# Attention and FFN in one kernel: 12 FFN chunks of 384 tokens instead of 9 of 512, four PSUM work banks, and another order of the attention's steps

## The chip, the cores and the metric

One core of one Trainium2 chip runs the whole kernel. The metric is the device time of one launch in microseconds, less being better. The core has TensorE (PE in the profile; PEld is its weight load), VectorE (DVE), ScalarE (ACT), GpSimd (POOL) and SyncE (SP), which issues all the DMAs here. Matrix products go to PSUM, eight banks of 512 float32 per partition.

## The reference

```
# q, k, v: (8 batches, 8 heads, 576 positions, 64); blocks of 64 positions
scores = q @ k^T / 8;  masked where block(row) < block(column)
attn = exp(scores - max); attn = attn / (sum + 1e-9)
x = (attn @ v) as (4608 tokens, 512)
h = x @ w_in                                  # w_in (512, 2048)
g = h if h >= 1, 0 if h <= -1, else (h + 1)^2 / 4
out = g @ w_out                               # w_out (2048, 512)
```

All of it is float32. The kernel computes with float32r operands and splits a float32 value into a high and a low part where it wants more precision: a product is then the sum of two or three matmuls (high x high, low x high, high x low).

## The kernel before

**Attention.** A `Pair` is two heads of one batch; there are 32 pairs, four to a batch. `attention_steps` walks over them in eight steps each, and every step ends with a `yield`. A pair needs `scores(j, g)` for its two heads j and three groups g of query rows (matmuls into a work bank, VectorE's maximum, ScalarE's exponential with its sum, VectorE's reciprocal and scaling), `scores_last` for the last 64 rows of both heads, `turn` and `turn_last` (TensorE transposes of the probabilities, then a copy to a high and a subtraction to a low part), and three parts of attn*v: `attn_v_first` for the first 256 rows of both heads, `attn_v(0)` and `attn_v(1)` for the rest. `add_halves` adds the two halves of a result (ScalarE copy, VectorE addition), and `store_x` writes x, split in high and low, into a ring of 1,536 tokens, `xh` and `xl`. From batch 1 on (`hop`) the probabilities go through a DMA, `as_float32r`, to a second buffer `prr` before they are turned; there are three buffers of the tag `bits` for that. From batch 2 on (`far`, also `raw`) an old pair's last parts run in the first steps of the next pair, and q and k come by way of `fetch` (a copy in DRAM), `load_qk`, `turned` and `turned_last` (TensorE transposes and `parted`). Batches 0 and 1 (`plain`) use plain float32 for attn*v and another order of steps, the `else` branches.

**FFN.** `feed_forward` goes over chunks of `TCH` = 512 tokens and, in each, over 16 slices `fc` of the hidden dimension. `ffn_in` makes one slice of h: 12 matmuls into the single bank `ph`, then ScalarE `t`, VectorE `t` twice, ScalarE `gh`, GpSimd `gl`, and a DMA of the slice of w_out, `wo`. `ffn_out` adds that slice to `po`, one bank for each 128 tokens: 8 matmuls with `gh` (L794) and 4 with `gl` (L799). The order is in(0), in(1), out(0), in(2), out(1) and so on; each of these is called an FFN block here. Two `wo`, `gh` and `gl` buffers exist.

**Order.** The main loop at the end runs the attention's steps; from step `START` = 36 on it issues one FFN block after each step, and when the attention is over, the rest of the blocks. `prepare_weights` converts the weights from float32 to their two parts, 64 pieces, in the early steps: 24 pieces by step 36 and the others in the 24 steps after it. The tile framework makes the instruction streams from this program order: it takes program order as priority and lets an instruction pass another that is not ready by its own estimate, which is why an attention transpose stands inside an `out` block in places. Each engine then runs its stream in order, and waits on semaphores.

**PSUM.** `ps_w` has 3 banks (`work_bank`: scores, transposes, attn*v), `ps_h` 1 (`ph`), `ps_o` 4 (`po`). Until step 36 `work_bank` also uses the `po` banks, every other time.

## Time and profile before

| | |
|---|---|
| median of 3 runs | 1270.7 us (1269.4 to 1272.47) |
| profiled execution | 1269.69 us, span 1267.9 us |
| mean granted TensorE clock | 0.981 |
| TensorE busy | 1200.1 us, 6280 matmuls |
| VectorE, ScalarE, GpSimd busy | 887.0, 703.2, 394.6 us |
| chain that ended last | PE 69%, DVE 16%, ACT 6%, issue 5% |
| DMA | 215.43 MB, mean 170 GB/s |

The profile is of one execution. Its parts are busy times, 40 slices of the span, the chain of work that ended last, groups of instructions by line and shape (busy us, mean ns of one, idle before it and what ended that), and DMA issues. A timeline row gives start, duration, engine, line, operation, result and operands, shape, count, and in brackets the idle time before it with its releaser. The ends of matmuls are modelled, so that two matmuls in a row overlap in the records; the distance between two starts shows how fast they go. A wait row says who waited for whom, us in total, times, and the longest.

### The profile page before, as it was taken

The numbers are of one execution on the slowest core, as the hardware profiler recorded it, in microseconds if no ns is written. First come the engines' busy times: TensorE is split into PE (matmuls) and PEld (weight loads), VectorE is DVE, ScalarE is ACT, GpSimd is POOL, SyncE is SP. The second block draws the span as 40 slices with busy tenths as digits, with TensorE's granted clock in tenths as the row PEclk, the third lists the DMA queues.
The fourth block names the chain that finished last, engine by engine and source line by source line (L and its number), as shares of the span: only waits on it lengthen the run. The fifth ranks groups of instructions, "written<-read, shape, count | busy, mean of one in ns | idle before, by whom it ended". The sixth has DMA issues, their size and how long they took to land.

```text
span 1267.9 us, 20253 instructions
## 1 busy us (share of the span) xinstructions
PE 1200.1 (95%) x6280; PEld 998.8 (79%) x6280; DVE 887.0 (70%) x2188; ACT 703.2 (55%) x1827; POOL 394.6 (31%) x430
## 2 busy tenths in 40 slices
PE   5888889899999999999999999999999999999998
PEld 4666667678888888888888888888888888888886
DVE  8898877758777777777777777787777777322222
ACT  5787656646566655665656655566556555222222
POOL 3555655522222222222222222222222222222222
PEclk9888988999999999999999999999999999999999
DMA  5566666667888655555554655465556433422432
GB/s 158 167 176 215 203 228 197 217 198 237 260 273 266 215 162 158 154 175 163 156 162 145 187 157 152 138 189 153 160 154 190 137 128 118 132 87 98 133 100 100
DMA packets 185259, 215.43 MB, mean 170 GB/s; under 512 B 113840, under 2 KB 132272, under 8 KB 184384
## 3 DMA queue, kind: packets, MB, share of 16 engines
q1 hardware_dynamic: 185152, 214.14, 54.9%
q8 instruction: 50, 0.82, 0.3%
q14 instruction: 57, 0.47, 0.1%
HBM read 134.74 MB, written 31.98 MB: 131 GB/s over the span
## 4 chain that ended last, share of the span: by engine, by line
PE 69%; DVE 16%; ACT 6%; issue 5%; DMA 1%; POOL 1%; SPq 1%; ACTq 0%; POOLq 0%; DVEq 0%
PE ph L770 29%; PE po L794 15%; PE po L799 7%; PE ps_av L591 7%; PE ps_s L482 4%; ACT pr L509 3%; PE ps_s L485 3%; DVE t L780 2%; PE ps_t L552 2%; DVE t L783 2%; ACT t L779 2%; DVE pb L547 2%; DVE nm L505 2%; DVE sm L491 1%; DVE pr L515 1%
## 5 line engine op out<-in xcount | busy, mean ns | idle before, releaser
L785 POOL TENSOR_TENSOR gl<-t,gh 128x512 fp32r<-128x512 f32 x144 | 187.5, 1302 | 510.2 <-ACT gh L784 333.2
L794 PE MATMUL po<-wo,gh 128*128 128x512 f32 x1152 | 296.1, 397 | 0.5 <-DMA wo<-wo_split 0.3
L794 PEld LDWEIGHTS po<-wo,gh 128*128 128x128 f32 x1152 | 212.5, 189 | 44.5 <-DMA wo<-wo_split 0.7
L770 PE MATMUL ph<-xh,wih 128*128 128x512 f32 x576 | 232.9, 404 | 1.6 <-DVE t L783 1.6
L770 PE MATMUL ph<-xh,wil 128*128 128x512 f32 x576 | 228.8, 397 | 0.0
L770 PE MATMUL ph<-xl,wih 128*128 128x512 f32 x576 | 227.8, 396 | 0.5 <-DVE xl L627 0.5
L780 DVE SCALAR_TENSOR_TENSOR t<-t 128x512 f32<-128x512 f32 x144 | 101.5, 705 | 168.0 <-ACT t L779 165.2
L779 ACT ACTIVATE t<-ph 128x512 f32<-128x512 f32 x144 | 85.9, 597 | 173.8 <-PE ph L770 173.8
L509 ACT ACTIVATE pr<-ps_s,nm 128x128 f32<-128x128 f32 (+3 forms) x256 | 134.1, 527 | 60.5 <-DVE nm L505 58.4
L784 ACT CAST gh<-t 128x512 fp32r<-128x512 f32 x144 | 89.5, 621 | 120.3 <-DVE t L783 120.0
L799 PE MATMUL po<-wo,gl 128*128 128x512 f32 x576 | 155.6, 392 | 0.0
L482 PE MATMUL ps_s<-ka,qa 68*128 68x288 f32 (+4 forms) x384 | 135.3, 367 | 15.0 <-ACT pr L509 5.4
L379 POOL TENSOR_TENSOR vsr<-vn,vsr 128x256 fp32r<-128x256 f32 (+1 forms) x96 | 55.2, 576 | 246.2 <-ACT vsr L378 244.6
L770 PEld LDWEIGHTS ph<-xh,wil 128*128 128x128 f32 x576 | 109.5, 190 | 23.8
L770 PEld LDWEIGHTS ph<-xh,wih 128*128 128x128 f32 x576 | 109.8, 191 | 21.7 <-DVE t L783 2.3
L799 PEld LDWEIGHTS po<-wo,gl 128*128 128x128 f32 x576 | 108.7, 189 | 23.1
L505 DVE TENSOR_REDUCE nm<-ps_s 128x1 f32<-128x128 f32 (+3 forms) x256 | 118.8, 482 | 10.4 <-PE ps_s L485 9.4
L770 PEld LDWEIGHTS ph<-xl,wih 128*128 128x128 f32 x576 | 109.7, 190 | 20.5 <-DVE xl L627 0.9
L485 PE MATMUL ps_s<-kb,qb 128*128 128x288 f32 (+4 forms) x384 | 121.1, 322 | 0.0
L515 DVE TENSOR_SCALAR pr<-pr,sm 128x128 f32<-128x128 f32 (+3 forms) x256 | 107.3, 440 | 5.4
L783 DVE TENSOR_TENSOR t<-ph,t 128x512 f32<-128x512 f32 x144 | 98.7, 686 | 2.2
L491 DVE TENSOR_SCALAR sm<-sm 128x1 f32<-128x1 f32 (+1 forms) x224 | 52.0, 232 | 68.3 <-ACT pr L509 65.7
(111 smaller groups left out, 1871.4 us busy)
## 6 DMA issues: line engine op xcount, KB each, us to landing
wo<-wo_split SPq DMA_DIRECT2D x144, 512.0 KB, 3.5
prr<-pr SPq DMA_DIRECT2D x96, 192.0 KB, 2.5
prr<-pr SPq DMA_DIRECT2D x72, 256.0 KB, 2.8
out_dram<-ob SPq DMA_DIRECT2D x36, 256.0 KB, 2.9
bits<-in_moe_w_in_dram SPq DMA_DIRECT2D x32, 256.0 KB, 3.5
bits<-in_moe_w_out_dram SPq DMA_DIRECT2D x32, 256.0 KB, 3.0
wo_split<-ws SPq DMA_DIRECT2D x16, 512.0 KB, 2.9
qa<-qb SPq DMA_DIRECT2D x63, 128.0 KB, 2.4
```

The source lines that it names most:

```text
L482: nc.tensor.matmul(ps, qa[:KA, j, c0 : c0 + P], ka[:KA, j, k0 : k0 + n], start=first, stop=False)
L485: nc.tensor.matmul(ps, qb[:, j, c0 : c0 + P], kb[:, j, k0 : k0 + n], start=False, stop=last)
L505: nc.vector.tensor_reduce(out=nm[:, i : i + 1], in_=ps[:, cs], axis=AX.X, op=ALU.max, negate=True)
L509: nc.scalar.activation(pr[:, cs], ps[:, cs], AF.Exp, bias=nm[:, i : i + 1], scale=1.0, accum_out=sm[:, i : i + 1],)
L515: nc.vector.tensor_scalar_mul(pr[:, cs], pr[:, cs], sm[:, i : i + 1])
L770: nc.tensor.matmul(ph, w[:, cc, fs], x[:, cc, xs], start=(cc == 0 and i == 0), stop=(cc == NCC - 1 and i == 2),)
L779: nc.scalar.activation(t_, ph, AF.Relu, bias=0.5, scale=0.5)
L780: nc.vector.scalar_tensor_tensor(out=t_, in0=t_, scalar=1.0, in1=t_, op0=ALU.min, op1=ALU.mult)
L783: nc.vector.tensor_tensor(out=t_, in0=ph, in1=t_, op=ALU.max)
L785: nc.gpsimd.tensor_tensor(out=gl, in0=t_, in1=gh.bitcast(F32), op=ALU.subtract)
L794: nc.tensor.matmul(po[tt], gh[:, ts_], wo[:, w, :], start=(fc == 0 and w == 0), stop=False)
L799: nc.tensor.matmul(po[tt], gl[:, ts_], wo[:, 0, :], start=False, stop=fc == NFC - 1)
```

## The change

- `TCH` is 384, so there are 12 chunks, `NTT` is 3, `ph` is 384 wide, and an `out` block has 6 + 3 matmuls; the ring keeps its length, 4 x 384. `BANK` = 512 takes the place of `TCH` where a bank's width was meant.
- `ps_o` has 3 banks, `ps_w` has 7 - 3 = 4.
- From batch 2 on a step starts with its scores and turns an older one afterwards; the DMA of the probabilities (`move`) is issued at the step's end; `attn_v(0)`, `attn_v_first` and `attn_v(1)` stand in steps 0, 1 and 2 of the next pair (before: `attn_v(0)` in step 7, then `attn_v_first` and `attn_v(1)` in steps 0 and 2). `turned_last` goes from the pair's own step 1 to step 5 of the pair before, and the corner of `turn_last` shares the bank of `turn(1, 0)` in step 7 instead of one of its own in step 6.
- The main loop issues one FFN block a step for the first 32 steps from 36 on, and then one and two in turn: two in the odd steps of a pair. The weight pieces follow the count of blocks, `due`, which is the count of steps while they last.

```diff
@@ -43,10 +43,11 @@
     NPAIR = H // 2
     NCC = DM // P
     NFC = DF // P
-    TCH = 512
+    TCH = 384
+    BANK = 512
     NCH = NT // TCH
     NTT = TCH // P
-    RING = 3 * TCH
+    RING = 4 * TCH
     G0 = 256
     G1 = S - G0
     SCALE = 1.0 / float(D) ** 0.5
@@ -71,7 +72,7 @@
     conv = ctx.enter_context(tc.tile_pool(name="conv", bufs=3))
     conv2 = ctx.enter_context(tc.tile_pool(name="conv2", bufs=3))
     dram = ctx.enter_context(tc.tile_pool(name="dram", bufs=1, space=bass.MemoryType.DRAM))
-    ps_w = ctx.enter_context(tc.tile_pool(name="ps_w", bufs=3, space=bass.MemoryType.PSUM))
+    ps_w = ctx.enter_context(tc.tile_pool(name="ps_w", bufs=7 - NTT, space=bass.MemoryType.PSUM))
     ps_h = ctx.enter_context(tc.tile_pool(name="ps_h", bufs=1, space=bass.MemoryType.PSUM))
     ps_o = ctx.enter_context(tc.tile_pool(name="ps_o", bufs=NTT, space=bass.MemoryType.PSUM))
 
@@ as_float32r: TCH becomes BANK (512) throughout, for example
-        for c0 in range(0, src.shape[1], TCH):
-            n = min(TCH, src.shape[1] - c0)
+        for c0 in range(0, src.shape[1], BANK):
+            n = min(BANK, src.shape[1] - c0)
...
@@ -513,7 +514,18 @@
             self.inverse(sm[:, :m])
             for i, cs in enumerate(cols):
                 nc.vector.tensor_scalar_mul(pr[:, cs], pr[:, cs], sm[:, i : i + 1])
-            self.pr[j, g] = as_float32r(pr[:, : cols[-1].stop], self.plain) if self.hop else [pr]
+            self.pr[j, g] = [pr[:, : cols[-1].stop]]
+            if not self.far:
+                self.moved(j, g)
+
+        def moved(self, *key):
+            if self.hop:
+                self.pr[key] = as_float32r(self.pr[key][0], self.plain)
+
+        def move(self, *key):
+
+            if self.far:
+                self.moved(*key)
 
         def scores_last(self):
 
@@ -539,7 +551,9 @@
             nc.vector.tensor_tensor(out=sm[:, 2:3], in0=sm[:, 0:1], in1=sm[:, 1:2], op=ALU.add)
             self.inverse(sm[:, 2:3])
             nc.vector.tensor_scalar_mul(pr, pr, sm[:, 2:3])
-            self.pr["last"] = as_float32r(pr, self.plain) if self.hop else [pr]
+            self.pr["last",] = [pr]
+            if not self.far:
+                self.moved("last")
 
         def split(self, ps, hi, lo=None):
             nc.scalar.copy(hi, ps)
@@ -547,7 +561,7 @@
                 nc.vector.tensor_tensor(out=lo, in0=ps, in1=hi.bitcast(F32), op=ALU.subtract)
 
         def transposed(self, out, parts, c0, n):
-            src = parts[c0 // TCH][:, c0 % TCH : c0 % TCH + n] if self.hop else parts[0][:, c0 : c0 + n]
+            src = parts[c0 // BANK][:, c0 % BANK : c0 % BANK + n] if self.hop else parts[0][:, c0 : c0 + n]
             if self.hop:
                 nc.tensor.transpose(out.bitcast(F32R), src, ident_r)
             else:
@@ -560,6 +574,8 @@
             ps = work_bank("ps_t")
             for c0 in range(0, n, P):
                 self.transposed(ps[:, c0 : c0 + P], pr, c0, P)
+            if self.far and j == 1 and g == 0:
+                self.turn_corner(self.pr.pop(("last",)), ps[:BLK, n : n + P])
             if g == 0:
                 self.split(ps[:, :n], *self.pa[j])
             else:
@@ -570,7 +586,7 @@
                 )
 
         def turn_last(self):
-            pr = self.pr.pop("last")
+            pr = self.pr["last",] if self.far else self.pr.pop(("last",))
             ps = work_bank("ps_t")
             for c0 in range(0, SM, P):
                 self.transposed(ps[:, c0 : c0 + P], pr, c0, P)
@@ -578,11 +594,13 @@
                 ps[:, :SM].rearrange("p (t h c) -> p t h c", h=2, c=BLK),
                 *(x[:, :, :, G1 - BLK :].rearrange("p h t c -> p t h c") for x in self.pb),
             )
-            ps = work_bank("ps_t")
-            self.transposed(ps[:BLK, :P], pr, SM, BLK)
-            self.split(
-                ps[:BLK, :P].rearrange("p (h c) -> p h c", h=2), *(x[:BLK] for x in self.pc)
-            )
+            if not self.far:
+                self.turn_corner(pr, work_bank("ps_t")[:BLK, :P])
+
+        def turn_corner(self, pr, ps):
+
+            self.transposed(ps, pr, SM, BLK)
+            self.split(ps.rearrange("p (h c) -> p h c", h=2), *(x[:BLK] for x in self.pc))
 
         def weighted(self, ps, j, parts, first=True, last=True):
             for i, (kt, lo_col, mov) in enumerate(parts):
@@ -605,11 +623,10 @@
                 parts.append((kt, lo_col, [x[:, j, kt, lo_col:] for x in self.pb]))
             return (*parts, (NTL, SM - G0, [x[:, j, :] for x in self.pc]))
 
-        def add_halves(self, ps, j, c0):
+        def add_halves(self, ps, j, c0, xtmp):
             main = slice(j * D, (j + 1) * D)
             rest = slice((1 - j) * D, (2 - j) * D)
             n = ps.shape[1]
-            xtmp = att1.tile([P, G1], F32, tag="xtmp", name="xtmp")
             nc.scalar.copy(xtmp[main, :n], ps[rest, :])
             nc.vector.tensor_tensor(
                 out=self.x32[main, c0 : c0 + n], in0=ps[main, :], in1=xtmp[main, :n], op=ALU.add
@@ -634,15 +651,16 @@
             ps = work_bank("ps_av")
             for j in range(2):
                 self.weighted(ps[:, j * G0 : (j + 1) * G0], j, self.parts_first(j))
+            xtmp = att1.tile([P, G1], F32, tag="xtmp", name="xtmp")
             for j in range(2):
-                self.add_halves(ps[:, j * G0 : (j + 1) * G0], j, 0)
+                self.add_halves(ps[:, j * G0 : (j + 1) * G0], j, 0, xtmp)
 
         def attn_v(self, j):
             if self.plain:
                 return self.both(G0, self.parts) if j else None
             ps = work_bank("ps_av")[:, :G1]
             self.weighted(ps, j, self.parts(j))
-            self.add_halves(ps, j, G0)
+            self.add_halves(ps, j, G0, att1.tile([P, G1], F32, tag="xtmp", name="xtmp"))
 
         def store_x(self):
 
@@ -675,82 +693,92 @@
             nxt = pairs[i + 1] if i + 1 < len(pairs) else None
             far = old is not None and old.far
             near = old is not None and not old.far
-            if far:
-                old.turn(1, 1)
             if cur:
                 cur.scores(0, 0)
                 cur.turned(False, 1)
                 cur.load("v")
             if far:
-                old.attn_v_first()
+                old.turn(1, 1)
+                old.attn_v(0)
             if near:
                 old.turn(1, 2)
+            if cur:
+                cur.move(0, 0)
             yield
+            if cur:
+                cur.scores(0, 1)
+                if not cur.raw:
+                    cur.turned_last()
+            if i + 2 < len(pairs):
+                pairs[i + 2].fetch()
             if far:
                 old.turn(1, 2)
-            if cur:
-                cur.scores(0, 1)
-                cur.turned_last()
-            if i + 2 < len(pairs):
-                pairs[i + 2].fetch()
+                old.attn_v_first()
             if near:
                 old.attn_v(1)
                 old.store_x()
+            if cur:
+                cur.move(0, 1)
             yield
             if far:
+                if cur:
+                    cur.scores(0, 2)
                 old.attn_v(1)
                 old.store_x()
-            if not cur:
-                return
-            if cur.far:
+                if not cur:
+                    return
+                if not cur.far:
+                    cur.begin()
+                    cur.turn(0, 0)
+            elif cur.far:
                 cur.scores(0, 2)
             else:
                 cur.begin()
                 cur.scores(0, 2)
                 cur.turn(0, 0)
+            cur.move(0, 2)
             yield
             if cur.far:
                 cur.begin()
+                cur.scores_last()
                 cur.turn(0, 0)
-                cur.scores_last()
             else:
                 cur.scores_last()
                 cur.turn(0, 1)
+            cur.move("last")
             if nxt:
                 nxt.load_qk()
                 nxt.split_q()
             yield
             if nxt:
                 nxt.split_k()
-            if cur.far:
-                cur.turn(0, 1)
-                cur.scores(1, 0)
-            else:
-                cur.scores(1, 0)
-                cur.turn(0, 2)
+            cur.scores(1, 0)
+            cur.turn(0, 1 if cur.far else 2)
+            cur.move(1, 0)
             if nxt:
                 nxt.turned(True, 0)
             yield
+            cur.scores(1, 1)
             if cur.far:
                 cur.turn(0, 2)
-                cur.scores(1, 1)
             else:
-                cur.scores(1, 1)
                 cur.turn_last()
+            cur.move(1, 1)
             if nxt:
                 nxt.turned(False, 0)
+                if nxt.raw:
+                    nxt.turned_last()
             yield
+            cur.scores(1, 2)
             if cur.far:
                 cur.turn_last()
-                cur.scores(1, 2)
             else:
-                cur.scores(1, 2)
                 cur.attn_v(0)
                 cur.turn(1, 0)
+            cur.move(1, 2)
             yield
             if cur.far:
                 cur.turn(1, 0)
-                cur.attn_v(0)
             else:
                 cur.turn(1, 1)
                 cur.attn_v_first()
@@ -762,7 +790,7 @@
 
     def ffn_in(c, fc):
         at = (c * TCH) % RING
-        ph = ps_h.tile([P, 512], F32, tag="ph", name="ph")
+        ph = ps_h.tile([P, TCH], F32, tag="ph", name="ph")
         fs = slice(fc * P, (fc + 1) * P)
         xs = slice(at, at + TCH)
         for cc in range(NCC):
@@ -834,14 +862,16 @@
     LAG = 2
     weights = prepare_weights()
     ffn_steps = feed_forward()
-    converted = 0
+    converted = done = 0
     for i, _ in enumerate(attention_steps()):
         if i < START:
             want = (i + 1) * EARLY // START
         else:
+
+            due = i - START + 1 + max(0, i - START + 1 - 2 * NFC) // 2
             want = max(
-                EARLY + (i - START + 1) * (NFC // GROUP * PART - EARLY) // (2 * NFC - 4 * GROUP),
-                ((i - START) // (2 * GROUP) + 1) * PART,
+                EARLY + due * (NFC // GROUP * PART - EARLY) // (2 * NFC - 4 * GROUP),
+                ((due - 1) // (2 * GROUP) + 1) * PART,
             )
         want += LAG
         for _ in range(want - converted):
@@ -849,7 +879,9 @@
         converted = max(converted, want)
         if i >= START:
             banks["free"] = False
-            next(ffn_steps, None)
+            for _ in range(due - done):
+                next(ffn_steps, None)
+            done = due
     for _ in ffn_steps:
         pass
 
```

More of the change, by code (lines that the diff above doesn't have):

```diff
@@ L234, in as_float32r @@
                 spare["of"] = [t_[:, :NTL, :, :].rearrange("p t h d -> p (t h d)") for t_ in vsr]
-                spare["of"].append(att1.tile([P, S], F32R, tag="x32", name="prs")[:, :TCH])
+                spare["of"].append(att1.tile([P, S], F32R, tag="x32", name="prs")[:, :BANK])
                 spare["end"] = att1.tile([P, G0 + P], F32R, tag="pa11", name="pre")[:, :BLK]
@@ L238, in as_float32r @@
             spare["n"] += 1
-            if src.shape[1] > TCH:
+            if src.shape[1] > BANK:
                 moved.append(spare["end"])
             for i, dst in enumerate(moved):
-                n = min(TCH, src.shape[1] - i * TCH)
-                nc.sync.dma_start(dst[:, :n].bitcast(F32), src[:, i * TCH : i * TCH + n])
+                n = min(BANK, src.shape[1] - i * BANK)
+                nc.sync.dma_start(dst[:, :n].bitcast(F32), src[:, i * BANK : i * BANK + n])
             return moved
         moved = []
-        for c0 in range(0, src.shape[1], TCH):
-            n = min(TCH, src.shape[1] - c0)
+        for c0 in range(0, src.shape[1], BANK):
+            n = min(BANK, src.shape[1] - c0)
             pool, tag = ((conv, "bits"), (conv2, "work"))[c0 > 0]
-            dst = pool.tile([P, TCH], F32R, tag=tag, name="prr")
+            dst = pool.tile([P, BANK], F32R, tag=tag, name="prr")
             nc.sync.dma_start(dst[:, :n].bitcast(F32), src[:, c0 : c0 + n])
```

## The prediction

> **What bounds the kernel now.** I read the page first: busy times, then the slices.
>
> ```profile
> PE 1200.1 (95%) x6280; PEld 998.8 (79%) x6280; DVE 887.0 (70%) x2188; ACT 703.2 (55%) x1827; POOL 394.6 (31%) x430
> ...
> PE   5888889899999999999999999999999999999998
> ...
> DVE  8898877758777777777777777787777777322222
> ...
> PEclk9888988999999999999999999999999999999999
> ```
>
> TensorE looks full from the ninth slice on, and VectorE falls to 2-3 tenths in the last six: there only the FFN is left. A busy TensorE need not be a full one, because records of pipelined matmuls overlap, so I read starts instead of durations. The timeline of TensorE in that tail:
>
> ```profile
> 1202.04 0.40 PE L770 MATMUL ph<-xh,wil 128*128 128x512 f32 x1
> 1202.27 1.98 PE L794 MATMUL po<-wo,gh 128*128 128x512 f32 x8
> 1204.09 1.08 PE L799 MATMUL po<-wo,gl 128*128 128x512 f32 x4
> 1205.00 0.39 PE L770 MATMUL ph<-xh,wih 128*128 128x512 f32 x1
> ```
>
> Twelve matmuls take 1205.00 - 1202.27 = 2.73 us, 0.2275 us each, though each record lasts 0.39. That is one FFN block (an `in` or an `out` block), and here nothing lies between blocks. Next the windows by stage. I cut them where the FFN starts (step 36), where its 32nd block ends (290.3, step 67) and where the attention ends (1082.1). I call the stages A, B, C and D:
>
> ```profile
> 0.00:88.00 88.00, 64.99 (x331) 53.05 (x332) 76.76 (x236) 63.78 (x191) 42.32 (x59) 0.92 0.59 169
> 88.00:290.30 202.30, 176.69 (x848) 137.81 (x846) 151.97 (x389) 122.09 (x346) 99.16 (x120) 0.92 0.66 209
> 290.30:1082.10 791.80, 777.68 (x4316) 659.29 (x4315) 608.81 (x1493) 473.63 (x1218) 209.17 (x218) 1.00 0.57 175
> 1082.10:1267.90 185.80, 180.69 (x793) 148.70 (x792) 49.48 (x73) 43.67 (x73) 43.99 (x34) 0.99 0.33 108
> ```
>
> Columns: length; busy us (instructions) of TensorE, its weight loads, VectorE, ScalarE, GpSimd; clock; DMA share; GB/s. In C there are 5.5 matmuls per us (4316 / 791.8) at full clock; in B 4.2 at 0.92. So C and D are limited by how fast TensorE issues, while B (202.3 us for 32 steps, 6.3 each, against 4.2 in C) waits for others: weight conversion and the attention of batch 1. The chain of waits over B:
>
> ```profile
> by line: PE ph L770 13.9%; PE ps_av L591 12.3%; issue 9.9%; POOL work L183 4.8%; PE po L794 4.0%; DVE work L177 3.8%; DVE t L780 3.4%; DVE pr L515 3.3%; DVE work L171 3.2%; DVE nm L505 2.9%; DVE work L174 2.7%; ACT pr L509 2.3%; DMA prs<-pr
> ```
>
> FFN matmuls are 13.9 + 4.0 = 17.9% of that chain, 36 us; the rest passes between all engines.
>
> **Part 1: chunks of 384.** `in` blocks stay 12 matmuls, now of 384 columns; `out` blocks become 9 of 512; 192 of each instead of 144. I need the start-to-start time at 384:
>
> ```profile
> 821.06 0.29 PE L485 MATMUL ps_s<-kb,qb 128*128 128x288 f32 x1
> ...
> 822.00 0.39 PE L770 MATMUL ph<-xh,wih 128*128 128x512 f32 x1
> ```
>
> Seven matmuls of 288 columns, each with new weights, take (822.00 - 821.06) / 7 = 0.134 each. Between (288, 0.134) and (512, 0.2275) the line gives 0.174 at 384; pure proportion would give 0.171. An `in` block: 12 x 0.174 = 2.09; an `out` block: 9 x 0.2275 = 2.05. FFN stream: 192 x 4.14 = 795 against 144 x 5.46 = 786: **+8 us**, all on the path. The Trainium skill ("TensorE: Matmul & The Clock Gate", Back-to-back issue gap) gives columns / 2.4 + 2.5 ns, which is 215.8 ns at 512 and 162.5 at 384; by that the stream would grow by 1.5 us only and the sum would come out 6 lower. The trace's 227.5 ns disagrees, so I keep the rows.
>
> The evacuation chain of `ph` (one bank) must fit in the next `out` block, which shrinks to 2.05 us. In the tail:
>
> ```profile
> 1256.64 0.40 PE L770 MATMUL ph<-xh,wil 128*128 128x512 f32 x1
> ...
> 1257.13 0.60 ACT L779 ACTIVATE t<-ph 128x512 f32<-128x512 f32 x1 [2.76 <-PE ph L770]
> 1257.77 0.69 DVE L780 SCALAR_TENSOR_TENSOR t<-t 128x512 f32<-128x512 f32 x1 [4.04 <-ACT t L779]
> ...
> 1258.49 0.69 DVE L783 TENSOR_TENSOR t<-ph,t 128x512 f32<-128x512 f32 x1
> ```
>
> It ends at 1259.18, 2.14 after the last matmul's record; the next `in` comes 0.42 later (1256.87 + 2.73 = 1259.60). At 384 the three operations take less by these groups (C stage):
>
> ```profile
> L547 DVE TENSOR_TENSOR pb<-ps_t,pb 128x512 fp32r<-128x512 f32 x59 | 40.5, 686 | 0.6
> L547 DVE TENSOR_TENSOR pa<-ps_t,pa 128x384 fp32r<-128x384 f32 x40 | 22.2, 555 | 17.8 <-ACT pa L545 17.8
> ...
> L545 ACT CAST pb<-ps_t 128x512 fp32r<-128x512 f32 x58 | 34.1, 588 | 3.0 <-PE ps_t L552 1.8
> L545 ACT CAST pa<-ps_t 128x384 fp32r<-128x384 f32 x40 | 19.0, 476 | 18.9 <-PE ps_t L552 18.9
> ```
>
> Minus 0.13 twice on VectorE and 0.11 on ScalarE: 1.77 against 2.56 - 0.68 = 1.88 of cover. It fits by 0.1; if not, 0.1 x 32 = 3 us in the tail. In C an attention part (0.65 us or more) adds to the cover. Wider: 48 more groups of five evacuation instructions, and 48 more `wo` loads of 512 KB (25 MB), 285 blocks instead of 190 in C: 47 x 0.52 MB over 840 us adds 29 to 175 GB/s, DMA share about 0.66. `wo` lands in
>
> ```profile
> wo<-wo_split SPq DMA_DIRECT2D x144, 512.0 KB, 3.5
> ```
>
> 3.5 us and has at least an `in`, an `out`, an `in` and an attention part, about 6.5 us, less what it stands on SP's queue behind a `move` that waits for VectorE. I cost it at nothing (bound 3 us: one batch, 24 blocks, each 0.125 late). The copies of `po` at a chunk's end lie beside the next `in`: two on VectorE (0.69 each, as its other 512-column reads) against 2.09. A chunk's first `in` still comes in the step after `store_x` at the earliest, now behind an `out`: nothing. In A, where `po` banks serve the attention too, the two alternating rings change from 4 and 3 banks to 3 and 4: nothing.
>
> **Part 2: the pace.** The first 32 blocks still take one step each, then 1.5 blocks a step. At step 257, 222 blocks were issued before; now 317 of 384. The tail keeps 67 blocks of 2.07 = 139 us against 66 x 2.73 = 180. That is no gain by itself: C and D are both issue-bound, so work moved from D to C costs the same there. But B sheds 32 x (2.73 - 2.07) = 21 us of matmuls which C must take: **+21**, minus what B shortens. Bounds: 0 (conversion sets B) and 21 (TensorE sets it). From the chain: a quarter of 36 us is 9, and the shorter evacuations on it about 1: **-10**.
>
> **Part 3: four banks and the moved steps** (batches 2 to 7, 24 pairs of 8 x 791.8 / 190 = 33.3 us). Two recurring stalls in C:
>
> ```profile
> 812.49 0.34 PE L485 MATMUL ps_s<-kb,qb 128*128 128x384 f32 x1
> 813.21 0.25 PE L442 MATMUL ps_qk<-ident_r,qk 128*128 128x128 f32 x1 [0.38 <-DVE x L614]
> ...
> 397.59 0.51 PE L552 MATMUL ps_t<-ident_r,prr 128*128 128x128 f32 x5
> 398.42 0.50 PE L482 MATMUL ps_s<-ka,qa 68*128 68x512 f32 x1 [0.33 <-ACT pr L509]
> ```
> ```profile
> PE ps_qk L442 <- DVE x L614: 8.9, 23, 0.4
> ...
> PE ps_s L482 <- ACT pr L509: 5.4, 18, 0.3
> ```
>
> Both wait for a work bank, the first for the two halves of attn*v, the second for the exponential. Start to start they cost 0.72 - 0.18 = 0.54 (23 times: 12.4) and 0.83 - 0.34 - 0.07 = 0.42 (17 times: 7.1). With a fourth bank, `turned_last` two steps after its load and away from attn*v, and scores right after an FFN block, the bank asked for was filled a step earlier. **-19.5**; bounds 0 and -19.5.
>
> Order inside a step: the first score pair after attn*v or transposes is slower than after the FFN:
>
> ```profile
> 191.07 0.39 PE L482 MATMUL ps_s<-ka,qa 68*128 68x512 f32 x1
> 191.31 0.40 PE L485 MATMUL ps_s<-kb,qb 128*128 128x512 f32 x1
> ...
> 195.85 0.46 PE L770 MATMUL ph<-xh,wih 128*128 128x512 f32 x1
> 196.16 0.39 PE L770 MATMUL ph<-xl,wih 128*128 128x512 f32 x1
> ...
> 817.35 0.47 PE L482 MATMUL ps_s<-ka,qa 68*128 68x512 f32 x1
> 817.67 0.40 PE L485 MATMUL ps_s<-kb,qb 128*128 128x512 f32 x1
> ```
>
> 0.32 against 0.24: 0.08 for seven scores, 0.56 a pair gained. The price: the FFN block now always follows transposes or attn*v, and its first matmul takes 0.31 instead of 0.23, in four more steps of eight: 0.32. Net 0.24 x 24 = **-6**. The `move`s go to the end of their step, behind the `v` load, `fetch` and `load_qk` on SP; a score is still turned three steps later, over 10 us, against a hop of
>
> ```profile
> prr<-pr SPq DMA_DIRECT2D x72, 256.0 KB, 2.8
> ```
>
> 2.8 us: nothing, and without that cover one bank stall's price again. The corner's own bank, one request in 22 per pair, goes; its two copies stay.
>
> **Sum**: +8 + 21 - 10 - 19.5 - 6 = -6.5. The profiled execution took 1269.7 us (span 1267.9), 1.0 under the median 1270.7 of the three runs; from that median, 1264.
>
> **Rivals.**
> B gives everything back: another -11, **1253**. For it: B's TensorE is busy 176.7 of 202.3 us. Against it: VectorE is at 75% there, conversion is untouched.
> B gives nothing back: +10, **1274**. For it: three converting engines on its chain.
> VectorE becomes the bound in single-block steps (the case on the other side). Steps 4 to 6 carry two scores, two turns and both parts of the next q/k. Before, one such step holds VectorE for this long:
>
> ```profile
> 626.71 0.61 DVE L505 TENSOR_REDUCE nm<-ps_s 128x1 f32<-128x128 f32 x2
> ...
> 631.04 0.55 DVE L505 TENSOR_REDUCE nm<-ps_s 128x1 f32<-128x384 f32 x1
> ```
>
> 4.3 us, where the new step 4 lasts about 3.1: one `out`, and 11 short ones of the pair's 86 attention matmuls, which share 33.3 - 21.8 = 11.5 us (estimate: 1.0). If the 1.2 us lag is not fully caught up in step 5 (two blocks), the `in` of step 6 waits for `ph`: 0.55 us a pair makes +13, **1277**; from 0.27 a pair the gain is gone. Against it: over a pair VectorE is 77% busy (608.81 / 791.8), and step 5 lasts 5 us.
> The banks do not remove the stalls (the change does not do what it says): +19.5, **1284**. Against it: both rows name a bank's last reader.
> The clock falls in B, with TensorE idler: it is 0.92 in B and also 0.92 in A, which has no FFN, so I expect no fall; all the way to the lowest digit of the slices (8; taken as 0.89) it would be 3% of 177, +5, **1269**. The Trainium skill (same page, Part 1: The HAM clock gate) says that an idle window of about 3.4 us halves the clock, which would speak against thinning the FFN; the 0.92 of both stages bears out that gating happens, not that it would grow.
>
> **How the numbers follow.** Forecast 0.42, B all back 0.17, B nothing back 0.15, VectorE 0.13, banks 0.08, clock 0.05. A measurement here tells 0.2%, 2.5 us. Faster: nearly all of the first two, 0.58. Same: the clock case, half of "nothing back", the forecast's edge, 0.18. Slower: 0.24. The range 1252 to 1277 takes in the first three and most of the fourth case and leaves out the banks case and the ends. The likeliest case alone spans 1259 to 1268.
>
> **What would show it.** FFN blocks of 2.09 and 2.05 us in the tail with `in` following `out` at once; no L442 wait on L614 and no L482 wait on L509; the 32nd block ending near 280, the attention about 1120; a pair in C of 33.3 + 12 x 2.07 - 8 x 2.73 - 1.05 = 35.2 us. I am wrong if B stays at 202 us, or if `ph` waits for L783 in C.

## The result and the profile after

The changed kernel takes **1311.95 us** (median of 4 runs, 1310.32 to 1314.02) where the kernel before takes 1270.5 beside it: a ratio of 1.035, 95% interval 1.033 to 1.0368. The forecast was 1264 with a range up to 1277, so it missed the sign and, by 48 us, the size. The profiled execution has a span of 1310.4 us against 1267.9, at a mean granted clock of 0.98 in both.

The page of the changed kernel: busy times, and the chain that ended last, by engine.

```profile
PE 1217.2 (93%) x6856; PEld 1080.2 (82%) x6856; DVE 949.8 (72%) x2290; ACT 711.5 (54%) x1917; POOL 402.6 (31%) x478
...
PE 50%; DVE 33%; ACT 6%; issue 4%; DMA 3%; POOL 1%; SPq 1%; DVEq 0%; POOLq 0%; ACTq 0%
```

The busy share of TensorE hardly moved (93% after 95%). The chain did: VectorE's share of it doubled, 16% to 33%, and TensorE's fell from 69% to 50%.

The windows, with the same stages as before. The 32nd FFN block ends at 277.1 and the attention at 1164.1.

```profile
0.00:88.00 88.00, 64.44 (x339) 53.27 (x339) 76.52 (x234) 63.35 (x190) 41.99 (x59) 0.90 0.59 171
88.00:277.10 189.10, 153.65 (x790) 128.38 (x789) 145.61 (x386) 117.87 (x342) 92.73 (x119) 0.91 0.67 211
277.10:1164.10 887.00, 857.86 (x5029) 774.60 (x5027) 686.28 (x1600) 494.52 (x1315) 232.58 (x266) 1.00 0.61 187
1164.10:1310.40 146.30, 141.28 (x706) 123.92 (x704) 41.34 (x73) 35.77 (x71) 35.32 (x35) 1.00 0.41 135
```

B is 13.2 us shorter and D 39.5 (185.8 to 146.3), both near the forecast. C is 95.2 longer, 791.8 to 887.0, and C is where the forecast failed: it wanted the attention to end near 1120. The tail shows the FFN's own pace:

```profile
1244.12 0.36 PE L798 MATMUL ph<-xh,wih 128*128 128x384 f32 x1
1244.32 0.34 PE L798 MATMUL ph<-xl,wih 128*128 128x384 f32 x1
...
1246.06 0.34 PE L798 MATMUL ph<-xh,wil 128*128 128x384 f32 x1
1246.23 1.55 PE L822 MATMUL po<-wo,gh 128*128 128x512 f32 x6
1247.62 0.84 PE L827 MATMUL po<-wo,gl 128*128 128x512 f32 x3
1248.30 0.37 PE L798 MATMUL ph<-xh,wih 128*128 128x384 f32 x1
```

(1246.06 - 1244.32) / 10 is 0.174 a matmul, as interpolated; the blocks take 2.11 and 2.07 (forecast 2.09 and 2.05), and `in` follows `out` at once. So the stream of Part 1 is near the forecast, and it doesn't make the loss.

TensorE's waits inside C (from 300 to 1060 us; all tables of waits and groups below are of this window), us in total, times, longest, in the changed kernel; the two bank waits of before are gone, and this has come:

```profile
PE ph L798 <- DVE t L811: 21.9, 31, 1.1
PE ps_qk L402 <- DVE ka L447: 1.2, 2, 0.6
```

`ph` waits for L811, which is the old L783: the sentence "I am wrong if ... `ph` waits for L783 in C" is what happened.

For a sum over C I take, for every two matmuls in a row, the distance of their starts less the pure pace (0.2275 us at 512 columns, 0.174 at 384, 0.134 at 288, pro rata between), and call the sum TensorE's lost time. What pace the narrower matmuls are given shifts all totals below alike, by up to 7 us, and leaves their differences. It was 68.2 us before and is **92.7** now; the forecast wanted 68.2 - 25.5 = 42.7. The change of the span is then split up: B -13.2, FFN stream and blocks moved out of B +29 at the pure pace (the 8 and 21 of the prediction), lost time in C +24.5, in the tail +2.3: together +42.6 against 1310.4 - 1267.9 = 42.5. As lost time is whatever exceeds the pace, this sum has to close; that the pace is right is shown by the tail's blocks.

**Where TensorE waits.** Of the 92.7 us, 24.5 stand in one place, 23 times 1.06 us: at the start of the `in` block of a pair's step 6. The changed kernel, VectorE, ScalarE and TensorE in steps 5 and 6 of one pair:

```profile
732.69 0.34 PE L798 MATMUL ph<-xh,wih 128*128 128x384 f32 x1
...
734.26 1.55 PE L822 MATMUL po<-wo,gh 128*128 128x512 f32 x6
...
734.39 0.69 DVE L561 TENSOR_TENSOR pb<-ps_t,pb 128x512 fp32r<-128x512 f32 x1
...
734.97 0.48 ACT L807 ACTIVATE t<-ph 128x384 f32<-128x384 f32 x1
735.12 0.28 DVE L390 SCALAR_TENSOR_TENSOR qb<-ps_qk,qb 64x128 fp32r<-64x128 f32 x1
...
735.82 0.42 DVE L516 TENSOR_SCALAR pr<-pr,sm 128x384 f32<-128x384 f32 x1
736.15 0.55 DVE L808 SCALAR_TENSOR_TENSOR t<-t 128x384 f32<-128x384 f32 x1
...
736.74 0.29 DVE L396 TENSOR_TENSOR kb<-ps_qk,kb 64x128 fp32r<-64x128 f32 x1
...
737.04 0.28 DVE L447 TENSOR_SCALAR qa<-ps_qk 64x128 fp32r<-64x128 f32 x1
737.34 0.29 DVE L447 TENSOR_SCALAR ka<-ps_qk 64x128 fp32r<-64x128 f32 x1
737.66 0.56 DVE L811 TENSOR_TENSOR t<-ph,t 128x384 f32<-128x384 f32 x1
...
738.28 0.44 PE L798 MATMUL ph<-xh,wih 128*128 128x384 f32 x1 [1.01 <-DVE t L811]
738.56 0.34 PE L798 MATMUL ph<-xl,wih 128*128 128x384 f32 x1
```

Read VectorE's queue from top to bottom. ScalarE has `t` ready at 735.45, but VectorE is still behind with `qb`, the scaling and the rest, and takes L808 only at 736.15. That `qb` is already of `turned_last`, which the change put into step 5; its `kb`, `qa` and `ka` stand ahead of L811: 737.66 - 736.74 = 0.92 us. L811 releases `ph` at 738.22, and `in` starts 1.01 us late. The cover was one `out` of 2.07 us and a step's attention part, and it is short by about those three instructions.

**Why VectorE is late at all.** VectorE instructions beside GpSimd ones (POOL), the changed kernel:

```profile
572.14 1.43 POOL L675 TENSOR_TENSOR xl<-x,xh 128x576 fp32r<-128x576 f32 x1 [1.14 <-ACT xh L674]
572.49 1.50 DVE L808 SCALAR_TENSOR_TENSOR t<-t 128x384 f32<-128x384 f32 x1 [1.13 <-ACT t L807]
...
726.14 1.01 POOL L813 TENSOR_TENSOR gl<-t,gh 128x384 fp32r<-128x384 f32 x1 [2.06 <-ACT gh L812]
726.20 0.97 DVE L545 TENSOR_TENSOR nm<-nm 128x1 f32<-128x1 f32 x1
```

L808 takes 0.55 us in the rows above and 1.50 here, ending 0.42 after `xl`. `nm`, the smaller of two columns of one element, takes 0.97 us and ends with `gl` (727.15 and 727.17). I call such a stretch a hold. The groups of VectorE in C, first of the changed kernel, then of the one before (busy us, mean ns):

```profile
L808 DVE SCALAR_TENSOR_TENSOR t<-t 128x384 f32<-128x384 f32 x122 | 85.5, 701 | 57.8 <-ACT t L807 56.0
L545 DVE TENSOR_TENSOR nm<-nm 128x1 f32<-128x1 f32 x20 | 19.4, 970 | 0.0
L516 DVE TENSOR_SCALAR pr<-pr,sm 128x512 f32<-128x512 f32 x41 | 30.2, 737 | 1.4
```
```profile
L780 DVE SCALAR_TENSOR_TENSOR t<-t 128x512 f32<-128x512 f32 x91 | 62.9, 691 | 26.3 <-ACT t L779 23.9
L491 DVE TENSOR_SCALAR sm<-sm 128x2 f32<-128x2 f32 x45 | 22.5, 501 | 22.3 <-ACT pr L509 22.3
L491 DVE TENSOR_SCALAR sm<-sm 128x1 f32<-128x1 f32 x114 | 17.5, 154 | 38.9 <-ACT pr L509 36.6
L533 DVE TENSOR_TENSOR nm<-nm 128x1 f32<-128x1 f32 x23 | 3.7, 159 | 0.8
L515 DVE TENSOR_SCALAR pr<-pr,sm 128x512 f32<-128x512 f32 x46 | 22.7, 494 | 1.6
```

`t<-t` became no shorter with a quarter fewer columns (701 ns after 691), and `nm` went from 159 to 970 with the same shape: 23 times of 24 it now starts beside a `gl`. In C, `t<-t` starts 27 times beside `xl` or `vsr`, and each time ends no earlier than they do; of the other 116 none is over 0.56 us. The scaling of 512 columns, which has one operand besides its factors, is held 23 times of 47, beside `vsr`: 0.98 us instead of 0.49. Of the instructions with an operand in PSUM (L811, L561, the maxima) none is stretched so. As the excess of VectorE I sum up over C what an instruction lasts beyond the shortest of its operation and shape in the two kernels, where that is over 0.1 us: 15.7 us before, nearly all of it `sm` of two columns, and 65.5 after (`t<-t` 19.8, `nm` 18.8, the scalings of 512 and 384 columns 21.9). The Trainium skill ("SBUF — State Buffer", Who interferes with whom) says that a VectorE instruction with two SBUF inputs contends with a GpSimd instruction that reads SBUF, and that one in a two-port mode does too, where whoever issues first keeps the other out for its whole length. These rows agree with it.

### The profile page after: what moved, and what is told of

The parts are those of the page before. It is cut to its first block, busy times and chain, and to the rows that moved or that the text cites. A ratio compares the mean times of both kernels' runs of the same rounds, so it can differ in the third digit from the quotient of the medians.

```text
span 1310.4 us, 21877 instructions
## 1 busy us (share of the span) xinstructions
PE 1217.2 (93%) x6856; PEld 1080.2 (82%) x6856; DVE 949.8 (72%) x2290; ACT 711.5 (54%) x1917; POOL 402.6 (31%) x478
## 4 chain that ended last, share of the span: by engine, by line
PE 50%; DVE 33%; ACT 6%; issue 4%; DMA 3%; POOL 1%; SPq 1%; DVEq 0%; POOLq 0%; ACTq 0%
PE ph L798 19%; PE po L822 12%; PE ps_av L609 6%; PE po L827 6%; DVE t L808 4%; DVE pr L516 4%; DVE nm L506 4%; DVE t L811 3%; DVE pb L561 2%; PE ps_s L483 2%; PE ps_t L566 2%; PE ps_s L486 2%; DVE qb L390 2%; DVE kb L396 2%; DVE nm L541 2%
## 5 line engine op out<-in xcount | busy, mean ns | idle before, releaser
L813 POOL TENSOR_TENSOR gl<-t,gh 128x384 fp32r<-128x384 f32 x192 | 195.5, 1018 | 688.1 <-ACT gh L812 556.3
L798 PE MATMUL ph<-xh,wih 128*128 128x384 f32 x768 | 273.2, 356 | 46.0 <-DVE t L811 45.0
L798 PE MATMUL ph<-xl,wih 128*128 128x384 f32 x768 | 260.4, 339 | 1.8 <-DVE xl L644 1.8
L798 PE MATMUL ph<-xh,wil 128*128 128x384 f32 x768 | 260.4, 339 | 0.0
L808 DVE SCALAR_TENSOR_TENSOR t<-t 128x384 f32<-128x384 f32 x192 | 129.5, 674 | 177.0 <-ACT t L807 174.9
L812 ACT CAST gh<-t 128x384 fp32r<-128x384 f32 x192 | 98.5, 513 | 204.9 <-DVE t L811 204.3
L807 ACT ACTIVATE t<-ph 128x384 f32<-128x384 f32 x192 | 93.8, 488 | 129.0 <-PE ph L798 127.3
L811 DVE TENSOR_TENSOR t<-ph,t 128x384 f32<-128x384 f32 x192 | 105.9, 551 | 3.0
L561 DVE TENSOR_TENSOR pb<-ps_t,pb 128x512 fp32r<-128x512 f32 (+1 forms) x120 | 76.0, 634 | 21.1 <-ACT pb L559 20.5
L559 ACT CAST pb<-ps_t 128x512 fp32r<-128x512 f32 (+1 forms) x120 | 65.3, 544 | 29.0 <-PE ps_t L566 25.2
```

Source lines behind the costliest of these rows:

```text
L561: nc.vector.tensor_tensor(out=lo, in0=ps, in1=hi.bitcast(F32), op=ALU.subtract)
L798: nc.tensor.matmul(ph, w[:, cc, fs], x[:, cc, xs], start=(cc == 0 and i == 0), stop=(cc == NCC - 1 and i == 2),)
L808: nc.vector.scalar_tensor_tensor(out=t_, in0=t_, scalar=1.0, in1=t_, op0=ALU.min, op1=ALU.mult)
L811: nc.vector.tensor_tensor(out=t_, in0=ph, in1=t_, op=ALU.max)
L813: nc.gpsimd.tensor_tensor(out=gl, in0=t_, in1=gh.bitcast(F32), op=ALU.subtract)
```

## The experiments

Theory: C loses its time because the chain behind `ph` (L807 on ScalarE, L808 and L811 on VectorE) no longer fits the short single blocks, and it doesn't for two reasons, the place of `turned_last` and the holds by GpSimd. Rivals: 384 tokens cost it whatever the order (more blocks, more `wo`); the order costs it whatever the size; four banks bring nothing. All ratios are to the kernel before on the same chip (1267 to 1268 us there), with the 95% interval. Lost time and excess are those of C, taken from each run's one profile.

**e1. Less GpSimd work.** Changed kernel; the low parts of v and of x are copies on ScalarE, so the low parts are left out.

```diff
-                    nc.gpsimd.tensor_tensor(out=vs[...], in0=vn[...], in1=hi..., op=ALU.subtract)
+                    nc.scalar.copy(vs[...], vn[...])
...
-                nc.gpsimd.tensor_tensor(out=xl[...], in0=self.x32[...], in1=hi..., op=ALU.subtract)
+                nc.scalar.copy(xl[...], self.x32[...])
```

> The changed kernel, but from batch 1 on the low parts of v (vsr) and of x (xl, in store_x) are not subtracted on GpSimd: ScalarE copies a value there instead (left out: the subtraction). GpSimd keeps gl alone. Theory G (GpSimd holds VectorE up: a VectorE operation that reads two operands from SBUF starts its row and does not end before the GpSimd operation beside it has ended): VectorE's excess over its own shortest durations falls in the middle stage from 65 us to under 35, the wait of the in block of step 6 for ph from 1.2 to under 0.5 us a pair, time 1275 to 1290. Theory L (VectorE has simply too much work in steps 4 to 6 for the shorter steps, its durations being a side effect): the excess falls too, but the wait for ph stays at 1 us a pair or more and the time above 1300.

Measured: 1285.68 us, 1.0134 [1.0112, 1.0155]; lost time in C 67.1, VectorE's excess 8.1. The group that stood at 701 ns:

```profile
L806 DVE SCALAR_TENSOR_TENSOR t<-t 128x384 f32<-128x384 f32 x126 | 70.2, 557 | 63.3 <-ACT t L805 63.1
```

Taking this work from GpSimd returns 2.1% of the 3.5%, and `t<-t` has the 0.56 us that the prediction worked out. Time and excess are as theory G had them. The step-6 wait is not: it only falls to 17.6 us, 0.77 a pair, where G wanted it under 0.5.

**e2. Two blocks in the even steps** of a pair instead of the odd ones.

```diff
-            due = i - START + 1 + max(0, i - START + 1 - 2 * NFC) // 2
+            due = i - START + 1 + (max(0, i - START + 1 - 2 * NFC) + 1) // 2
```

> The changed kernel with the two FFN blocks in the even steps of a pair (0, 2, 4, 6) instead of the odd ones; nothing else. Theory L: steps 4 and 6, the loaded ones, now last 5 us each, the wait for ph goes (under 0.3 us a pair), time 1270 to 1285. Theory G: the clashes of xl and vsr in steps 2 and 3 do not depend on it; the excess of VectorE stays at 50 us or more and the time at 1300 or above, or it shifts by chance.

Measured: 1275.35 us, 1.0054 [1.0035, 1.0072]; lost time 56.7, excess 53.2, as theory L had it. One rounding in the pace returns 3.0 of the 3.5%. VectorE is held nearly as long as in the changed kernel, but `ph` hardly waits for it any more:

```profile
PE ph L798 <- DVE t L811: 2.2, 6, 0.5
```

**e3. The old order of steps** with 384 tokens, four banks and the same pace (the diff's hunks from `scores` to `attention_steps` undone).

> Chunks of 384, four work banks and the pace of one and two blocks, with the attention's steps in the order of before (turn before scores, attn*v in steps 7, 0 and 2, turned_last in the pair's own step 1). If the new order of steps is the cause (its store_x beside the evacuation, turned_last added to step 5): 1265 to 1280, no wait for ph over 0.3 us a pair. If the smaller chunks with the alternating pace are (theory L in its general form): 1295 or more.

Measured: 1274.36 us, 1.0035 [1.0014, 1.0056]; lost time 52.7, excess 40.5. In C, TensorE waits for VectorE at `ph` no more than this, and neither bank wait of before is there:

```profile
PE ph L771 <- DVE t L784: 0.8, 3, 0.3
```

So 384 tokens and the pace don't make the loss by themselves. Nor do the holds on `t<-t`, which are all here, 23 times beside `xl`:

```profile
L781 DVE SCALAR_TENSOR_TENSOR t<-t 128x384 f32<-128x384 f32 x128 | 88.8, 694 | 35.9 <-ACT t L780 32.9
```

In the old order `ph` is free in time all the same. Lost time fell by 68.2 - 52.7 = 15.5 us against the kernel before. I put that down to the four banks, as the two waits that are gone were for banks; the chunks and the pace changed with them.

**e4. The new order alone:** 512 tokens, three banks, one block a step.

```diff
-    TCH = 384
+    TCH = 512
-    RING = 4 * TCH
+    RING = 3 * TCH
-            due = i - START + 1 + max(0, i - START + 1 - 2 * NFC) // 2
+            due = i - START + 1
```

> The new order of the attention's steps alone: chunks of 512, three work banks, one block a step as before. If the new order is the cause: VectorE's excess in the middle stage well above the 16 us of before, and 1285 or more. If chunks and pace are: no wait for ph, as each block lasts 2.73 us, and 1255 to 1275 (the old bank waits may partly return with three banks).

Measured: 1272.83 us, 1.0036 [1.0023, 1.0049]; lost time 72.5, excess 45.1. No wait at `ph`, but another:

```profile
PE ps_qk L443 <- DVE kb L396: 14.8, 21, 0.8
```

`turned_last` in step 5 asks for a bank whose last reader is the copy of `kb` of the step before. The order alone costs little too, where "1285 or more" was expected if it were the cause. It is the order together with the short chunks and their pace that costs 3.5%.

**e5. Changed kernel, `turned_last` in step 7** instead of 5.

```diff
             if nxt:
                 nxt.turned(False, 0)
-                if nxt.raw:
-                    nxt.turned_last()
...                                            # at the end of step 7
+                if nxt.raw:
+                    nxt.turned_last()
```

> The changed kernel (two blocks in odd steps) with turned_last of the next pair in step 7 instead of step 5: its four VectorE operations, 1.15 us together, leave the stretch of steps 4 to 6, nothing else changes. Theory L (too much VectorE work in steps 4 to 6): the wait before the in block of step 6, 1.07 us a pair now, falls under 0.3 and the time to 1278 to 1290. Theory G (the clashes with GpSimd in steps 2 and 3 make VectorE late, the load later on does not matter): the excess of VectorE stays near 65 us, the wait above 0.7, the time above 1298.

Measured: 1286.2 us, 1.015 [1.012, 1.018]; lost time 67.4, excess 64.6. The holds are all there, and the wait at `ph` is down to

```profile
PE ph L798 <- DVE t L811: 3.9, 14, 0.5
```

`turned_last` in step 5 is thus the direct cause of the step-6 wait: without it lost time at that place falls from 24.5 to some 6 us. (The edit moves all of it: the three instructions ahead of L811, the `qb` ahead of L808, two copies on ScalarE and a transpose.)

**e6. e2 with e1's edit** (the low parts left out as there).

> Two blocks in even steps (as in the run with even steps, 1275) and no subtractions of vsr and xl on GpSimd (left out, ScalarE copies instead): what do the clashes cost once the wait for ph is gone? If VectorE is off the path there (theory L): 1272 to 1277, though its excess falls from 53 us to under 15. If its lateness still costs in other waits (theory G): 1260 to 1270.

Measured: 1267.77 us, 1.000 [0.9987, 1.0013]; lost time 48.6, excess 13.1, in theory G's range. With the even pace the same edit still returns 0.5%, against 2.1% with the odd one: the price of the holds depends on the slack.

**e9. The changed kernel with one operand in PSUM.** The minimum-and-product reads `ph` instead of `t` as its second operand; the activation is another function then (its square is left out).

```diff
-            out=t_, in0=t_, scalar=1.0, in1=t_, op0=ALU.min, op1=ALU.mult
+            out=t_, in0=t_, scalar=1.0, in1=ph, op0=ALU.min, op1=ALU.mult
```

> The changed kernel, but VectorE's min-and-multiply of an `in` block (`t<-t`) takes its second operand from `ph` in PSUM instead of `t` in SBUF (so the activation function is another one: this leaves out the square). Theory: a VectorE operation with two operands in SBUF is held while GpSimd works, and with one in PSUM it is not. Then the group's mean falls from 674 ns to 540-570 ns, with hardly any of it over 0.7 us, that is 0.11 x 192 = 21 us less VectorE time, most of it inside the chain that frees `ph`; the waits of `ph` for VectorE shrink and the time falls by 8 to 20 us against the changed kernel (ratio to before 1.019 to 1.029). Rival 1 (these operations are long because of something else, for example a slow ScalarE or DMA traffic into SBUF): mean stays above 640, time 1308-1312 (1.033 to 1.037). Rival 2 (the hold just passes on to the next operations, which then meet the same GpSimd instruction): the mean falls, others such as `pr` scaling grow, time falls by less than 5 us.

Measured: 1290.28 us, 1.019 [1.0162, 1.0217]; lost time 72.6, excess 46.0 (the profiled execution, 1295.91, is the longest of its four). GpSimd's work, the blocks and the order are those of the changed kernel:

```profile
L808 DVE SCALAR_TENSOR_TENSOR t<-t,ph 128x384 f32<-128x384 f32 x125 | 69.1, 553 | 58.6 <-ACT t L807 56.0
L545 DVE TENSOR_TENSOR nm<-nm 128x1 f32<-128x1 f32 x21 | 20.4, 972 | 0.0
```

701 ns became 553 by the operand's place alone: in C 28 of these start beside `xl` or `vsr`, and none is over 0.56 us. `nm`, still with both in SBUF, stays at 972. It returns 1.6%, some 20 us, for about 148 ns x 125 = 18.5 us less work on VectorE in these 760 us. The first theory's numbers held; the rivals (long for another reason, or the hold passes on to the next) are out, as the excess fell by these 19 us. The step-6 wait is still 23.6 us, so it does not come from the holds on `t<-t`; with most other holds gone too it fell to 17.6 (e1).

**Towards a better version.** e4's wait names its own cure: another place for `turned_last`. **e7**: e4 with it in step 7; **e8**: e4 with it at the end of step 6.

```diff
             if nxt:
                 nxt.turned(False, 0)
-                if nxt.raw:
-                    nxt.turned_last()
...                                            # e8, at the end of step 6 (e7: of step 7)
+            if nxt and nxt.raw:
+                nxt.turned_last()
```

> Chunks of 512, three work banks, one block a step, the new order of steps, but turned_last in step 7. The run with the new order alone had one big wait in the middle stage, 20 us for a bank whose reader is VectorE's kb, in step 5, at turned_last. If that wait is the only thing between the new order and a gain: 1248 to 1260. If the wait only moves to another request for one of three banks: 1265 or more.

> The same with turned_last at the end of step 6, where the bank it takes over was filled a step earlier than in step 5: 1248 to 1260 if that is enough, 1265 or more if VectorE is late there too (step 6 then holds its 1.2 us beside a scores of 512 columns and a turn).

Measured: e7 1263.3 us, 0.9967 [0.9949, 0.9986], lost time 62.2, between its two cases; e8 **1254.1 us, 0.9891 [0.9869, 0.9913]**, lost time 55.3, as hoped for. TensorE's largest wait in C, first of e7, then of e8:

```profile
PE ps_av L609 <- DVE ka L447: 6.4, 19, 0.4
```
```profile
PE ps_t L566 <- PE ps_s L486: 2.7, 6, 0.5
```

In step 7 `turned_last` delays the next pair's attn*v, in step 6 nothing in particular. e8 beats both kernels with 512 tokens and three banks.

**e10. e8 with e1's edit** (low parts left out).

> The order with scores first, 512 tokens and `turned_last` at the end of step 6 (1254.1, ratio 0.989), with the low parts of v and x as ScalarE copies instead of GpSimd subtractions (so the low parts are left out). If holds by GpSimd still cost time there: 1245-1251, 0.982-0.987. If VectorE's lateness is hidden with blocks of 2.73 us in every step: no change, 0.987-0.992. VectorE's excess over its own shortest durations falls from 45 us to about 15 either way.

Measured: 1254.66 us, 0.9904 [0.9888, 0.9921]; excess 24.5 after e8's 45.1. Not faster than e8: with 2.73 us of block in every step the holds that the edit removes cost nothing. The excess was expected at 15. Of what is left, 19.8 us are `sm` of two columns, which starts beside a `gl` all 47 times (mean 585 ns); the edit leaves `gl` as it is, so this hold's price stays open.

**e11. 384 tokens and four banks with both mends** (e2's pace and e8's place).

> 384 tokens and four banks, two blocks in the even steps of a pair and `turned_last` in step 6: both mends of the pace and the place at once. If 384 tokens cost what the prediction's first two parts say (+8 for the stream and +10 for what stage B sheds) and four banks bring no more than three: 1254 + 18 = 1272, ratio 1.003. If four banks do bring something over three: 1262-1268, 0.994-1.000. If the two mends only repeat each other (two blocks in even steps alone was 1.0054): 1275, 1.005.

Measured: 1276.81 us, 1.0074 [1.0059, 1.0089]; lost time 55.5. All three cases had it lower; it is nearest to the third, that the two mends only repeat each other (e2 alone 1.0054). Lost time is that of e8, which has one bank less. Against e8 384 tokens cost 1.8%, 23 us, where the prediction's first two parts make 8 + 21 - 10 = 19.

**e12. The kernel before, with `turned_last` alone moved** to the end of step 6 of the pair before.

```diff
-                cur.turned_last()
+                if not cur.raw:
+                    cur.turned_last()
...                                            # at the end of step 6, from batch 2 on
+                if nxt:
+                    nxt.turned_last()
...                                            # and in the branch of batches 0 and 1
+                if nxt and nxt.raw:
+                    nxt.turned_last()
```

> The kernel before with one thing moved: `turned_last` of the raw pairs goes from the pair's own step 1 to the end of step 6 of the pair before; order of scores and turns, 512 tokens and three banks as before. If the gain of 13 us in the 512-token version with scores first is the removed wait of `ps_qk` for attn*v (12.4 us): 1254-1258, ratio 0.989-0.992. If scores first is what brings it and the move only avoids a new wait: 1264-1268, 0.997-1.000. If it takes another step's bank instead (step 6 also turns and scores): 1268-1272, 1.000-1.003.

Measured: 1270.8 us, 1.003 [1.0019, 1.0041]; lost time 71.5. The wait for attn*v's halves is gone, the one for the exponential stays, and small new ones have come:

```profile
PE ps_s L482 <- ACT pr L509: 5.3, 17, 0.4
PE ps_qk L401 <- DVE ka L446: 3.6, 16, 0.2
PE ps_av L591 <- DVE kb L395: 2.3, 6, 0.4
```

The move alone gains nothing, as the third case expected; the order alone (e4) gains nothing either. Together they gain 1.1%.

## Why the prediction was wrong, point by point

- **Part 1, +8: right.** The tail's blocks are 2.11 and 2.07 us, each 0.02 over the forecast. The Trainium skill ("TensorE: Matmul & The Clock Gate", Back-to-back issue gap) gives columns / 2.4 + 2.5 ns, by which 162.5 ns at 384 columns would be the estimate; the tail's rows show 174.
- **Part 2, +21 and -10: right.** The 21 is arithmetic, and B shortened by 13.2.
- **Part 3, four banks, -19.5: right in kind, some 4 too high.** In the old order (e3) lost time fell by 15.5, and both waits named are gone.
- **Part 3, order inside a step, -6: this is the step that failed.** It counted only TensorE's pace after one kind of matmul or another, and put at nothing what the new order asks of VectorE. The pace itself came near: by the sums over C, the second matmuls of the score pairs are late by some 13 us less than before (forecast 13.4), and the FFN blocks' first matmuls cost 9.6 more (forecast 7.7). But going from the old to the new order at 384 tokens (e3 to the changed kernel) raised lost time by 40 us, 52.7 to 92.7, of which 24 stand in step 6, where `ph` waits for VectorE. And even where `ph` hardly waits (e11), order, place and banks together bring 12.7, not 25.5, no more than four banks in the old order (15.5, e3). With three banks (e8) the order and a good place bring the same 12.9, and both waits of before are gone there too; beside that order no gain of a fourth bank is seen.
- **The move of `turned_last` was counted on TensorE's side only** ("two steps after its load and away from attn*v"). Its `qb`, `kb`, `qa` and `ka` are VectorE's, and VectorE takes its queue in order: 0.92 us of them stand ahead of L811, with `ph` waiting behind it and TensorE behind `ph`. That an evacuation chain "fits by 0.1" in the tail was no cover in C, where VectorE's queue is not empty.
- **The rival named the place, not the price.** "The `in` of step 6 waits for `ph`" is word for word what the trace shows. It had 0.55 us a pair and a chance of 0.13; the wait is 1.06 a pair, and the holds come on top. Its argument against, VectorE 77% busy over a pair, is an average; in the rows of steps 5 and 6 VectorE is busy without a gap.
- **The holds were not seen**, though the trace of before shows them: 501 ns for `sm` 128x2 against 154 for 128x1 is no price of one more column (all 47 in C start beside a `gl` and end with it or after it). The duration of `t<-t` was scaled with its columns, from rows that met no GpSimd work; the shorter blocks moved it beside `xl` and, twice, `vsr`. In the changed kernel the price by e9 is some 20 us; in e3, with the same holds in the old order, none is seen at `ph`.

The 50 us between 42.7 and 92.7 in C, then: 24.5 for the step-6 wait, about 20 for the holds on `t<-t` (e9), and 12.8 in short delays that the even pace keeps too (e11's 55.5 less 42.7). That is 57, so the parts overlap by some 7. How far the two causes feed each other stays open: e5 and e9 were not run together.

## What to carry to other kernels

When a step is moved, write its instructions into the queue of every engine that runs them, and look what stands behind each: a release that others wait for (here L811) must not follow work that nobody is waiting for. A rhythm of short and long steps has its slack in the long ones, so put the evacuation-heavy steps there; one rounding was worth 3% here. And two edits that remove the same wait are worth it once.

## What the runs showed of the hardware

- A VectorE instruction with both operands in SBUF that starts beside a GpSimd one ends with it or after it: 0.97 us instead of 0.16 for one column (`nm`, 23 of 23 in C), 1.50 instead of 0.55 for 384 (`t<-t`, 27 of 27). The scaling of `pr` from SBUF to SBUF is held as well (0.98 instead of 0.49 at 512 columns), and so is the one-operand `sm` of two columns (501 ns), but not `sm` of one column (154 ns). With one operand in PSUM `t<-t` kept 553 ns (e9).
- The group's mean hides it when a shorter shape should have been faster: 691 ns at 512 columns, 701 at 384. Compare a group with the shortest of its own kind, not with the group of before.
- Such holds cost what the slack leaves. Taking two of GpSimd's three jobs away returned 2.1% in the odd pace (e1), 0.5% in the even one (e6 against e2), and nothing with 512 tokens (e10, 0.9904, against e8, 0.9891).
